# Output by pairs of batches: seven tokens of a run on one partition, one DMA for a pair, in an attention and soft-MoE kernel

## The chip, the cores and the metric

The kernel runs on one core of one Trainium2 chip. The metric is the device time of one execution in microseconds (us); the figure given for a kernel is the median over its timed runs. The engines are named as in the profile: PE (TensorE, matmuls; PEld its weight loads), DVE (VectorE), ACT (ScalarE), POOL (GpSimd), SP (SyncE, which here does nothing but issue the output's DMAs). "Tile" is the library that lays out buffers and puts the waits between engines; the kernel asks it to keep the order of instructions as written.

## The reference

Attention over 8 batches, 12 heads, 448 tokens and a head size of 64, with a softmax that has an extra term in its denominator; then a soft mixture of experts over all 3,584 tokens with 8 experts of 4 slots each.

```python
scores = scale * np.matmul(q, k.transpose(0, 1, 3, 2))
m = np.max(scores, axis=-1, keepdims=True)
e = np.exp(scores - m)
attn = e / (np.sum(e, axis=-1, keepdims=True) + np.exp(-m) + 1e-09)
x = np.matmul(attn, v)             # then tokens to rows: [3584, 768]

logits = x @ phi                   # [3584, 32]
d = np.exp(logits - logits.max(0)) # over tokens
d /= d.sum(0, keepdims=True) + 1e-09
slot_input = (d.T @ x).reshape(E, S_per_e, D)
for e in range(E):
    h = np.maximum(slot_input[e] @ w1[e], 0.0)
    slot_out[e] = h @ w2[e]
c = np.exp(logits - logits.max(1)) # over slots
c /= c.sum(1, keepdims=True) + 1e-09
out = c @ slot_out                 # [3584, 768], float32, 11.01 MB
```

## The kernel before

**Tokens.** A batch's 448 tokens are 64 runs of 7 successive tokens: run p holds tokens 7p to 7p + 6. The seven are kept in four column groups. Groups 0, 1 and 2 have 128 columns: the first 64 are token i of each run (i = 0, 1, 2), the other 64 are token 4 + i. Group 3 has 64 columns, token 3.

**Main loop.** For 48 steps (8 batches of 6 pairs of heads, line 532 on) the kernel transposes q and k, takes row maxima (L226, L233), exponentials (L299), multiplies by v (L324), normalizes, and turns the result for the logits (L367 to L372). After the last pair of a batch the lambdas of `P(b)` run, spread over the next steps: logits, a running softmax over tokens into `acc`, and for the softmax over slots the step `c_turn` (L450 to L457). It transposes the exponentials `cd` of the batch, so that the slots lie on partitions (32 of them for each of the four groups: 128 partitions) and tokens on columns, copies that to `cT[:, b, :]` (L453), and leaves the reciprocal of each token's sum in `crec[:, b, 0:4]` (L455 to L457). `crec` has tokens on partitions: column i belongs to group i, rows 0 to 63 to the first 64 tokens of the group, rows 64 to 127 to the others. For the last batch this is `last[3]`, called after the hidden layers.

**Weights.** w1 and w2 of the experts, 16 pieces of 128 x 6144 bf16, are loaded on POOL's queue during the main loop: 11 into buffers of a pool `wpool` with 11 buffers (L594), five into parts of `R` whose contents are no longer needed.

**Experts.** After the main loop: `hidden(0)` and `hidden(1)` (L624, L626) for experts 0 to 3 and 4 to 7, `last[3]()`, `turn(0)`, `turn(1)` (transposes L631, copies L632), `slots(0)`, `slots(1)` (L639, copies L644 and L645), and a selection by masks (L664 to L669) which leaves in `slot_out` the 32 slots' outputs, four times, on partitions 0 to 31, 32 to 63 and so on. The tile `wt`, the buffer of the first expert's w1, holds these intermediates.

**Output (L672 to L695).** For each batch four PSUM tiles of two banks are taken, one for each token group. Eight matmuls (two halves of 384 columns, outer; four groups, inner) multiply `cT`'s 32 rows of a group by `slot_out`. Then the four tiles are scaled by `crec` into a buffer `o` in SBUF: groups 0 and 2 by ACT (L688), 1 and 3 by DVE (L690). Group 3 has 64 rows. So `o` has tokens 0 to 3 of run p on partition p, and tokens 4 to 6 on partition 64 + p. Two DMAs on SP's queue take a batch to the output: L694 from partitions 0 to 63 (four tokens, 12,288 contiguous bytes for each partition), L695 from partitions 64 to 127 (three tokens, 9,216 bytes). The first batch goes in two cuts of two and one or two tokens, so there are 18 DMAs. `o` takes the pool's buffers after `wt`: those that held w1 of experts 1 to 7 and w2 of expert 0. Tile gives the output's DMAs eight semaphores in turn; the ninth and later issues wait also for the landing of the eighth before.

Of the kernel before, what the change touches and what calls it, by code (L numbers as in the profile page):

```python
# [30 lines left out]
def kernel(  # L31
# [10 lines left out]
    nc = tc.nc  # L42
    B, H, S, D = q.shape
    DD = H * D
    NS = moe_phi.shape[1]
    E = moe_w1.shape[0]
    SE = NS // E
    F = moe_w1.shape[2]
    KC = DD // 128
    FK = F // 128  # L50
    ND = DD // 2
# [7 lines left out]

    const = ctx.enter_context(tc.tile_pool(name="const", bufs=1))  # L60
    keep = ctx.enter_context(tc.tile_pool(name="keep", bufs=1))
    wpool = ctx.enter_context(tc.tile_pool(name="wpool", bufs=11))


    cT = keep.tile([128, B, 128], BF16, name="cT")
    crec = keep.tile([128, B, 4], F32, name="crec")
    acc = keep.tile([128, KC + 1, NS], F32, name="acc")

# [1 line left out]
    identf = const.tile([128, 128], F32, name="identf")  # L70
# [27 lines left out]
    w_sb = {}  # L98
# [10 lines left out]
    def load_half(i, z, t=None):  # L109

        if t is not None:
            w_view(i, t)
        n = (KC if halves[i][0] == "w1" else FK) // 2
        load_part(i, z * n, (z + 1) * n)

    w_tile = lambda: wpool.tile([128, KC * F], BF16, tag="w", name="w_sb")
    for i in range(5):
        w_view(11 + i, R[:, i * KC * F:(i + 1) * KC * F])

    with ExitStack() as at:  # L120
# [6 lines left out]
        pb_ = lambda nm: psB.tile([128, 512], F32, tag="b", name=nm)  # L127
# [33 lines left out]
        for base in (0, 64):  # L161

            nc.gpsimd.affine_select(
                out=sel[base:base + 64], in_=sel[base:base + 64], fill=1.0,
# [215 lines left out]
        def P(b):  # L380
# [69 lines left out]
            def c_turn():  # L450
                ps = pa([128, 128], BF16, "ps_ct")
                nc.tensor.transpose(ps, flat(v["cd"][:, 0:4, :]), ident)
                nc.vector.tensor_copy(cT[:, b, :], ps)  # L453
                r = crec[:, b, :]
                nc.vector.reduce_sum(r, v["cd"][:, 0:4, :], axis=AX.X)  # L455
                nc.vector.tensor_scalar(r, r, 1e-9, None, op0=ALU.add)
                nc.vector.reciprocal(r, r)  # L457
# [36 lines left out]
        take = lambda z, n: ub[:, z:z + n]  # L494
# [2 lines left out]
        masks = [take(F + KC * NS + g * 4 * NS, 4 * NS).rearrange("p (r s) -> p r s", r=4) for g in range(2)]  # L497
        fold = take(F + (KC + 8) * NS, 2 * NS).bitcast(F32)
        hrec = psm.tile([128, 1], F32, name="hrec", bufs=1)
        last = P(B - 1)  # L500
        post[2 * NPAIR] = last[0]

# [25 lines left out]
        half_at = {s: i for i, s in enumerate((1, 4, 7, 10, 13, 16, 22, 25, 28, 31, 34))}  # L528
# [3 lines left out]
        for s in range(NPAIR + 1):  # L532
            for y in range(2):
                hs = 2 * s + y
                early = int(hs < 5)
                As(1)
                if s < NPAIR:
                    Bk(s, 2 * y)
                    As(early)
                    Bk(s, 2 * y + 1)  # L540
                As(1)
                if hs == 1:
                    W1(1)
                if hs < 5:
                    T(hs + 3)
                if y == 0:
                    if 0 <= s - 1:
                        for i in (2, 3):
                            AV(s - 1, i, range(3))
                else:  # L550
                    if 2 <= s < NPAIR - 6:
                        T(s + 6)
                    g = (s + 1) // 3
                    if (s + 1) % 3 == 0 and g < NG:
                        W2(g + 1)
                        W3(g + 1)
                    if s < NPAIR:
                        for i in (0, 1):
                            AV(s, i, range(3))
                if 2 * s + y in post:  # L560
                    post[2 * s + y]()
                if y and 0 <= s - 2 < NPAIR - 2:
                    PX(s - 2)
                if y == 0:
                    if 0 <= s - 1:
                        for i in range(4):
                            AV(s - 1, i, [3])
# [12 lines left out]
            g = (s + 9) // 3  # L580
            if s % 3 == 0 and g - 2 < NG:
                V(g - 2)
                if s and g - 1 < NG:
                    load(g - 1, "v")
            if s == 1 or (s and s % 3 == 0):
                if g < NG:
                    load(g, "q")
                    load(g, "k")
            if s % 3 == 1:
                if 1 < (s + 2) // 3 < NG:  # L590
                    W1((s + 2) // 3 + 1)
                if s == 1:
                    load(2, "v")
            if s in half_at:  # L594
                load_half(half_at[s], 0, w_tile())
            if s - 1 in half_at:
                load_half(half_at[s - 1], 1)
            for i, z0, z1 in part_at.get(s, ()):
                load_part(i, z0, z1)
# [7 lines left out]
        for g in range(2):  # L607

            nc.gpsimd.memset(masks[g], 0.0)
            o = masks[g][:, :, 16 * g:16 * g + 16].rearrange("p r (i k) -> p r i k", i=4)  # L610
# [17 lines left out]
        def turn(g):  # L628
            ps = psA.tile([128, FK, 128], BF16, tag="a", name="ps_ht")
            for kt in range(FK):  # L630
                nc.tensor.transpose(ps[:, kt, :], h[g][:, kt * 128:(kt + 1) * 128], ident)  # L631
            nc.vector.tensor_copy(hT[g], ps)  # L632

        def slots(g):
            pss = [pb_("ps_so") for _ in range(2)]
            for kt in range(FK):
                for half in range(2):
                    for i in range(4):
                        nc.tensor.matmul(pss[half][32 * i:32 * i + 32, 0:ND],  # L639
                                         hT[g][:, kt, 32 * i:32 * i + 32],  # L640
                                         w_sb["w2", 4 * g + i][:, kt, half * ND:(half + 1) * ND],
                                         start=(kt == 0), stop=(kt == FK - 1),
                                         skip_group_check=True)
            nc.scalar.copy(so[g][:, 0:ND], pss[0][:, 0:ND])  # L644
            nc.vector.tensor_copy(so[g][:, ND:DD], pss[1][:, 0:ND])  # L645

        hidden(0, h0)

        wt = w_tile()
        h1, so = wt[:, 0:F], [wt[:, 3 * F + g * DD:3 * F + (g + 1) * DD] for g in range(2)]  # L650
        h = [h0, h1]
        hT = [wt[:, (1 + g) * F:(2 + g) * F].rearrange("p (k s) -> p k s", k=FK) for g in range(2)]
        slot_out = wt[:, 3 * F + 2 * DD:3 * F + 3 * DD]
        hidden(1, h1)
        last[3]()
        turn(0)
        turn(1)
        slots(0)
        slots(1)
        for half in range(2):  # L660
            hs = slice(half * ND, (half + 1) * ND)
            ps = psA.tile([128, 512], F32, tag="a", name="ps_sel")
            for g in range(2):
                nc.tensor.matmul(ps[:, 0:ND], masks[g].rearrange("p r s -> p (r s)"), so[g][:, hs],  # L664
                                 start=(g == 0), stop=(g == 1))
# [3 lines left out]
                nc.scalar.copy(slot_out[:, hs], ps[:, 0:ND])  # L669


    with ExitStack() as ex:  # L672
        psO = ex.enter_context(tc.tile_pool(name="psO", bufs=4, space=PSUM))
        for b in range(B):
            o = wpool.tile([128, KC * F], BF16, tag="w", name="o_sb")[:, :].bitcast(F32)
            o = o.rearrange("p (i d) -> p i d", i=4)
            pss = [psO.tile([128, 2, 512], F32, tag="o", name="ps_o") for _ in range(4)]
            for half in range(2):
                for i in range(4):
                    m = 128 if i < 3 else 64  # L680
                    r = slice(32 * i, 32 * i + NS)
                    nc.tensor.matmul(pss[i][0:m, half, 0:ND], cT[r, b, 0:m],  # L682
                                     slot_out[r, half * ND:(half + 1) * ND], start=True, stop=True)
            for i in range(4):
                m = 128 if i < 3 else 64
                dst = o[0:m, i, :].rearrange("p (h d) -> p h d", h=2)
                if i % 2 == 0:
                    nc.scalar.mul(dst, pss[i][0:m, :, 0:ND], crec[0:m, b, i:i + 1])  # L688
                else:
                    nc.vector.tensor_scalar(dst, pss[i][0:m, :, 0:ND], crec[0:m, b, i:i + 1], None, op0=ALU.mult)  # L690
            ov = out[b * S:(b + 1) * S, :].rearrange("(p t) d -> p t d", t=7)
            cuts = [0, 2, 4] if b == 0 else [0, 4]
            for t0, t1 in zip(cuts, cuts[1:]):
                nc.sync.dma_start(out=ov[:, t0:t1, :], in_=o[0:64, t0:t1, :])  # L694
                nc.sync.dma_start(out=ov[:, 4 + t0:min(4 + t1, 7), :], in_=o[64:128, t0:min(t1, 3), :])  # L695


# [28 lines left out]
```

## Time and profile before

| what | us |
|---|---|
| median of 3 runs | 341.22 (340.12 to 342.4) |
| the profiled execution's own time | 341.64 |
| its span on the core | 339.9 |
| hidden layers end, turns of the last batch | about 291 |
| slots (L639) | 292.7 to 298.0 |
| first matmul of the output stage | 299.8 |
| first output DMA issued | 301.9 |
| last scaling ends | 324.7 |
| last output DMA issued, landed | 329.9, 338.6 |

A second table has the rows of the output stage and of the small steps before it, one instruction's mean from the groups of the profile:

| line | engine | what | count | mean ns |
|---|---|---|---|---|
| L682 | PE | 32 x 128 by 32 x 384 | 48 | 461 |
| L682 | PE | 32 x 64 by 32 x 384 | 16 | 500 |
| L688 | ACT | scaling, 128 x 768 | 16 | 897 |
| L690 | DVE | scaling, 128 x 768 | 8 | 1018 |
| L690 | DVE | scaling, 64 x 768 | 8 | 1001 |
| L453 | DVE | copy into cT, 128 x 128 | 8 | 224 |
| L457 | DVE | reciprocal, 128 x 4 | 8 | 178 |
| L632 | DVE | copy of a turned hidden layer, 128 x 1024 | 2 | 686 |
| L406 | PE | fp32 transpose, 128 x 128 | 8 | 325 |

The page's own list of DMA issues has the output in these groups (bytes of one, median us from issue to landing):

```profile
out_dram<-o_sb SPq DMA_DIRECT2D x7, 768.0 KB, 8.9
out_dram<-o_sb SPq DMA_DIRECT2D x7, 576.0 KB, 8.3
out_dram<-o_sb SPq DMA_DIRECT2D x3, 384.0 KB, 4.8
out_dram<-o_sb SPq DMA_DIRECT2D x1, 192.0 KB, 5.1
```

How to read such a profile: it is one execution. The page cuts the span into 40 equal slices and gives, for each engine, a digit for its busy share in tenths; PEclk is the granted clock of TensorE, DMA the mean busy share of the 16 DMA engines, GB/s what they moved. A timeline row has the start, the time, engine and line, the operation, the tiles out<-in with shapes, and in brackets how long the engine had been idle before it and what ended that. "SPq" is SP's sequencer, where a DMA's issue is recorded. A windows row gives the same sums for any stretch.

### The profile page before, as it was taken

To read this page: it belongs to the slowest core of one execution; us is meant where nothing else is said; L and a number is where in the kernel's file an instruction comes from. 1 tells how busy PE (TensorE), PEld (TensorE's weight loads), DVE (VectorE), ACT (ScalarE), POOL (GpSimd) and SP (SyncE) were. 2 spreads that over 40 slices of the span, in tenths; PEclk is the share of its full clock that TensorE was granted. 3 is DMA by queue.
4 is the path that set the end of the run, shared out by engine and by line. 5 is a ranking of instruction groups with operands and counts; after the bars stand their busy time and mean duration, and the time that the engine had idled before them with its cause. 6 is when DMAs were issued, how large, how long until landed. Compare 5 with 4: busy or idle time off the path is not lost.

```text
span 339.9 us, 12092 instructions
## 1 busy us (share of the span) xinstructions
PE 295.1 (87%) x5040; PEld 167.7 (49%) x5040; DVE 264.6 (78%) x609; ACT 253.5 (75%) x547; POOL 198.8 (58%) x399
## 2 busy tenths in 40 slices
PE   3898999999999999999999999999999868977800
PEld 1344556556564656555656555565645433522200
DVE  5789998989998999899989899998893563255520
ACT  2476799998999799889989998998899842255410
POOL 8742777969587777777785969586567350000000
PEclk9999999999999999999999999999999985975555
DMA  7990999999999999099999999997344999839996
GB/s 93 125 128 0 159 186 175 179 194 137 201 146 180 159 171 148 9 171 151 176 172 179 148 185 153 180 147 126 48 70 74 157 211 208 150 79 268 353 361 235
DMA packets 42870, 54.30 MB, mean 160 GB/s; under 512 B 2752, under 2 KB 35520, under 8 KB 41920
## 3 DMA queue, kind: packets, MB, share of 16 engines
q0 software_dynamic: 41376, 42.52, 81.4%
q1 hardware_dynamic: 1440, 11.01, 9.8%
q8 instruction: 39, 0.64, 0.7%
q14 instruction: 15, 0.12, 0.1%
HBM read 85.03 MB, written 11.01 MB: 283 GB/s over the span
## 4 chain that ended last, share of the span: by engine, by line
PE 43%; DVE 25%; ACT 12%; issue 6%; DMA 6%; POOL 3%; DVEq 0%; POOLq 0%; ACTq 0%
DVE mx L226 15%; PE ps_av L324 8%; PE ps_b L294 6%; PE ps_a L222 6%; DMA R<-in_k_dram 5%; ACT R L299 5%; PE ps_t L200 5%; PE ps_b L296 4%; PE ps_o L682 3%; ACT R L203 2%; PE ps_h L624 2%; ACT o_sb L688 2%; PE ps_s L447 2%; DVE mx L233 2%; ACT R L370 2%
## 5 line engine op out<-in xcount | busy, mean ns | idle before, releaser
L226 DVE TENSOR_REDUCE mx<-ps_a 128x1 f32<-128x448 f32 x288 | 160.8, 615 | 12.3 <-PE ps_a L222 11.1
L299 ACT ACTIVATE R<-ps_b 128x448 bf16<-128x448 f32 x336 | 157.9, 555 | 13.8 <-PE ps_b L296 9.3
L294 PE MATMUL ps_b<-R 64*128 64x448 bf16 (+1 forms) x384 | 82.2, 357 | 0.9 <-ACT R L370 0.2
L296 PE MATMUL ps_b<-mT,sel 64*128 64x448 bf16 (+1 forms) x384 | 78.2, 352 | 0.0
L222 PE MATMUL ps_a<-R 64*128 64x448 bf16 x288 | 68.6, 364 | 6.0 <-DVE mx L226 4.3
L349 POOL TENSOR_TENSOR R<-ubuf,rec 128x384 bf16<-128x384 f32 x44 | 36.2, 824 | 55.2 <-DVE rec L346 53.0
L324 PE MATMUL ps_av<-R 128*128 128x65 bf16 (+1 forms) x1536 | 64.5, 196 | 1.5 <-DVE ubuf L336 1.4
L324 PEld LDWEIGHTS <-R 128*128 128x128 bf16 (+1 forms) x1536 | 50.3, 100 | 28.0 <-issue 24.0
L200 PEld LDWEIGHTS <-R 64*64 64x64 bf16 x1344 | 30.3, 113 | 19.9 <-issue 8.6
L370 ACT CAST R<-ps_x 128x512 bf16<-128x512 f32 x47 | 28.0, 597 | 13.9 <-PE ps_x L367 13.9
L200 PE MATMUL ps_t<-ident,R 64*64 64x64 bf16 x1344 | 31.2, 196 | 7.9 <-DMA R<-in_q_dram 4.3
L294 PEld LDWEIGHTS <-R 64*128 64x128 bf16 (+1 forms) x384 | 19.2, 97 | 27.8 <-issue 23.1
L296 PEld LDWEIGHTS <-sel 64*128 64x128 bf16 (+1 forms) x384 | 21.1, 97 | 23.1 <-issue 15.6
L233 DVE TENSOR_REDUCE mx<-ps_a 128x1 f32<-128x448 f32 x48 | 29.8, 621 | 0.7 <-PE ps_a L231 0.5
L203 ACT COPY R<-ps_t 128x896 bf16<-128x896 bf16 x20 | 18.3, 916 | 11.3 <-PE ps_t L200 11.3
L336 ACT COPY ubuf<-ps_av 128x455 f32<-128x455 f32 x44 | 24.6, 560 | 1.8 <-PE ps_av L324 1.0
L222 PEld LDWEIGHTS <-R 64*128 64x128 bf16 x288 | 17.8, 94 | 14.6 <-issue 3.8
L682 PE MATMUL ps_o<-w_sb,cT 32*128 32x384 bf16 x64 | 18.2, 470 | 5.8 <-ACT o_sb L688 5.1
L690 DVE TENSOR_SCALAR o_sb<-ps_o,crec 128x768 f32<-128x768 f32 (+1 forms) x16 | 15.5, 1010 | 9.4 <-PE ps_o L682 9.4
L688 ACT ACTIVATE o_sb<-ps_o,crec 128x768 f32<-128x768 f32 x16 | 13.5, 897 | 11.5 <-PE ps_o L682 11.5
L355 POOL TENSOR_TENSOR R<-ubuf,rec 128x128 bf16<-128x128 f32 x44 | 17.6, 400 | 3.7
L367 PE MATMUL ps_x<-ident,R 128*128 128x128 bf16 x192 | 18.8, 219 | 0.4 <-DVE R L355 0.4
(115 smaller groups left out, 371.6 us busy)
## 6 DMA issues: line engine op xcount, KB each, us to landing
w_sb<-in_moe_w_dram POOLq DMA_DIRECT2D x22, 768.0 KB, 8.8
R<-in_v_dram POOLq DMA_DIRECT2D x32, 192.0 KB, 4.6
out_dram<-o_sb SPq DMA_DIRECT2D x7, 768.0 KB, 8.9
R<-in_q_dram POOLq DMA_DIRECT2D x15, 336.0 KB, 7.3
R<-in_k_dram POOLq DMA_DIRECT2D x15, 336.0 KB, 8.2
out_dram<-o_sb SPq DMA_DIRECT2D x7, 576.0 KB, 8.3
R<-in_moe_w_dram POOLq DMA_DIRECT2D x4, 768.0 KB, 8.3
R<-in_moe_w_dram POOLq DMA_DIRECT2D x1, 1344.0 KB, 13.1
```

What stands on the lines that cost most here:

```text
L200: nc.tensor.transpose(ps[r, a, c:c + 64], src[r, pl, tok * D:(tok + 1) * D], ident[r, r])
L203: nc.scalar.copy(t, ps)
L222: nc.tensor.matmul(pss[hl][:, 0:S], t[r, 0, i * 128:(i + 1) * 128], t[r, 1, :], start=True, stop=True)
L226: nc.vector.reduce_max(mx[g][:, c:c + 1], pss[hl][:, 0:S], axis=AX.X)
L233: nc.vector.reduce_max(mx[g][:, c:c + 1], ps[:, 0:S], axis=AX.X)
L294: nc.tensor.matmul(outs[hl], t[rs[hl], 1, cols], t[rs[hl], 0, :], start=True, stop=False)
L296: nc.tensor.matmul(outs[hl], sel[rs[hl], 2 * pl + hl:2 * pl + hl + 1].to_broadcast([64, m]), mT[mg(n)][rs[hl], :], start=False, stop=True)
L299: nc.scalar.activation(e, p[:, 0:S], AF.Exp, scale=scale)
L324: nc.tensor.matmul(o, eT[n, i, hl][:, qc], vp[g % 2][:, 2 * pl + hl, i, 0:W65], start=(i == 0 and u == 0 and hl == 0), stop=(i == 3), skip ...
L349: eng.tensor_mul(x[:, 0:3, c:c + 128].rearrange("p i (h d) -> p i h d", h=2), u[:, 0:6, 0:D].rearrange("p (i h) d -> p i h d", h=2), rec[: ...
L370: nc.scalar.copy(xT[:, pb, :], ps)
L682: nc.tensor.matmul(pss[i][0:m, half, 0:ND], cT[r, b, 0:m], slot_out[r, half * ND:(half + 1) * ND], start=True, stop=True)
```

## The change

`cT` is laid out by pairs of batches, `[128, 4 pairs, 2 halves of a group, 2 batches, 64 runs]`, so that for a token and a pair the 128 runs of the two batches are 128 successive columns. In the output loop, now over four pairs, token t of both batches is one matmul pair of 128 rows. A partition holds one run's seven tokens (21,504 contiguous bytes; partitions 0 to 63 the even batch, 64 to 127 the odd one), in a group of four and a group of three PSUM tiles. Tokens 0 to 3 use the rows of groups 0 to 3 and the first half of columns, tokens 4 to 6 those of groups 0 to 2 and the second half. One DMA of 128 partitions takes a pair out; the first pair goes in three cuts, of tokens 0 and 1, 2 and 3, and 4 to 6. There are 6 output DMAs instead of 18, 56 matmuls instead of 64, and 28 scalings instead of 32, all of 128 rows.

The reciprocals have then to lie with a pair's runs on partitions: four fp32 matmuls against an identity of 64 x 64 move `crec`'s quadrants into PSUM, and two copies take them to `cscale`, after `turn(1)` and before `slots(0)`.

The pool of 11 weight buffers becomes one tile `W` of 11 x 6144 columns with fixed slices; the output's pairs lie in it one behind the other from the second slice on.

```diff
-    wpool = ctx.enter_context(tc.tile_pool(name="wpool", bufs=11))
-    cT = keep.tile([128, B, 128], BF16, name="cT")
+    cT = keep.tile([128, B // 2, 2, 2, 64], BF16, name="cT")
...
-    w_tile = lambda: wpool.tile([128, KC * F], BF16, tag="w", name="w_sb")
+    W = keep.tile([128, 11 * KC * F], BF16, name="W")
+    w_tile = lambda i: W[:, i * KC * F:(i + 1) * KC * F]
...
-                nc.vector.tensor_copy(cT[:, b, :], ps)
+                nc.vector.tensor_copy(cT[:, b // 2, :, b % 2, :], ps.rearrange("p (h j) -> p h j", h=2))
...
+        cscale = take(F + (KC + 10) * NS, 8 * B).bitcast(F32).rearrange("p (h b i) -> p h b i", h=2, i=4)
...
         turn(1)
+        for half in range(2):
+            ps = pb_("ps_cs")
+            r = slice(64 * half, 64 * half + 64)
+            for b2 in range(2):
+                nc.tensor.matmul(ps[64 * b2:64 * b2 + 64, 0:2 * B], identf[r, r], crec[r, b2::2, :],
+                                 start=True, stop=True)
+            nc.vector.tensor_copy(cscale[:, half].rearrange("p b i -> p (b i)"), ps[:, 0:2 * B])
         slots(0)
...
+        for bp in range(B // 2):
+            o0 = KC * F + bp * 14 * DD
+            o = W[:, o0:o0 + 14 * DD].bitcast(F32).rearrange("p (t d) -> p t d", t=7)
+            ov = out[2 * bp * S:2 * (bp + 1) * S, :].rearrange("(p t) d -> p t d", t=7)
+            for t0, t1 in (0, 4), (4, 7):
+                pss = [psO.tile([128, 2, 512], F32, tag="o", name="ps_o") for _ in range(t0, t1)]
+                for hf in range(2):
+                    for t in range(t0, t1):
+                        r = slice(32 * (t - t0), 32 * (t - t0) + NS)
+                        nc.tensor.matmul(pss[t - t0][:, hf, 0:ND], cT[r, bp, t0 // 4, :, :].rearrange("p b j -> p (b j)"),
+                                         slot_out[r, hf * ND:(hf + 1) * ND], start=True, stop=True)
+                for t in range(t0, t1):
+                    dst = o[:, t, :].rearrange("p (h d) -> p h d", h=2)
+                    c = cscale[:, t0 // 4, bp, t - t0:t - t0 + 1]
+                    if t % 2 == 0:
+                        nc.scalar.mul(dst, pss[t - t0][:, :, 0:ND], c)
+                    else:
+                        nc.vector.tensor_scalar(dst, pss[t - t0][:, :, 0:ND], c, None, op0=ALU.mult)
+            cuts = [0, 2, 4, 7] if bp == 0 else [0, 7]
             for t0, t1 in zip(cuts, cuts[1:]):
-                nc.sync.dma_start(out=ov[:, t0:t1, :], in_=o[0:64, t0:t1, :])
-                nc.sync.dma_start(out=ov[:, 4 + t0:min(4 + t1, 7), :], in_=o[64:128, t0:min(t1, 3), :])
+                nc.sync.dma_start(out=ov[:, t0:t1, :], in_=o[:, t0:t1, :])
```

More of the change, by code (lines that the diff above doesn't have):

```diff
@@ L594 @@
             if s in half_at:
-                load_half(half_at[s], 0, w_tile())
+                load_half(half_at[s], 0, w_tile(half_at[s]))
             if s - 1 in half_at:
@@ L647 @@
         hidden(0, h0)
-        wt = w_tile()
+        wt = w_tile(0)
         h1, so = wt[:, 0:F], [wt[:, 3 * F + g * DD:3 * F + (g + 1) * DD] for g in range(2)]
@@ L673 @@
         psO = ex.enter_context(tc.tile_pool(name="psO", bufs=4, space=PSUM))
[L674 to L692, printed above, removed]
```

## The prediction

> **What bounds the kernel now.** I read four views in this order: the page's slices, the timeline of the end, the windows of the output stage, and the DMA issues with the trace's packet records. The slices first (40 slices of 8.5 us; the last five cover 297.4 to 339.9 us):
>
> ```profile
> PE   3898999999999999999999999999999868977800
> PEclk9999999999999999999999999999999985975555
> DMA  7990999999999999099999999997344999839996
> GB/s 93 125 128 0 159 186 175 179 194 137 201 146 180 159 171 148 9 171 151 176 172 179 148 185 153 180 147 126 48 70 74 157 211 208 150 79 268 353 361 235
> ```
>
> The change touches only the output stage and two small steps before it. In that stage TensorE runs at half clock and ends two slices before the span does, while the DMA digits read 9, 9, 9, 6. So the stage is to be read as a transfer of the output, and the question is what sets its rate: 79, 268, 353, 361, 235 GB/s.
>
> The timeline shows where the stage starts and what closes the span:
>
> ```profile
> 299.83 1.16 PE L682 MATMUL ps_o<-w_sb,cT 32*128 32x384 bf16 x8 [0.65 <-DVE w_sb L667]
> 301.94 0.52 SPq L694 DMA_DIRECT2D out_dram<-o_sb  x1
> 302.50 0.59 SPq L695 DMA_DIRECT2D out_dram<-o_sb  x1
> ...
> 322.73 1.69 ACT L688 ACTIVATE o_sb<-ps_o,crec 128x768 f32<-128x768 f32 x2 [1.44 <-PE ps_o L682]
> ...
> 329.93 1.74 SPq L695 DMA_DIRECT2D out_dram<-o_sb  x1
> ```
>
> The last eviction is over by 324.7 us, the last issue comes at 329.93 and lands at 338.59; 1.3 us of closing work follow, and the span is 339.9. From 324.7 on no engine computes. Making evictions cheaper would therefore gain nothing by itself; a faster drain, or bytes that start earlier, would.
>
> The windows (per row: start and end, length, busy time of PE, PEld, DVE, ACT, POOL, then clock, DMA share, GB/s) say why the drain is slow:
>
> ```profile
> 303.10:305.10 2.00, 1.47 (x7) 0.49 (x7) 1.14 (x2) 1.17 (x2) 0.00 (x0) 0.50 1.00 200
> 309.00:311.00 2.00, 1.62 (x6) 0.45 (x6) 0.80 (x2) 0.81 (x2) 0.00 (x0) 0.50 1.08 229
> 320.00:322.00 2.00, 1.30 (x5) 0.36 (x4) 1.56 (x2) 1.29 (x2) 0.00 (x0) 0.50 1.01 399
> 324.00:326.00 2.00, 0.00 (x0) 0.00 (x0) 0.70 (x1) 0.42 (x1) 0.00 (x0) 0.50 1.04 407
> ```
>
> All 16 DMA engines are busy in all four, yet the rate is 200, 229, 399 and 407 GB/s. The packet records (start, length and bytes of each packet) tell the difference. An output packet is one partition's run: 12,288 bytes from partitions 0 to 63 (L694), 9,216 from 64 to 127 (L695). Between 309.0 and 311.9 nearly all 16 packets in flight are of L694; each then takes 0.84 to 1.01 us, and together they make 203 GB/s in the microsecond at 310. With five or fewer of the other kind beside them the mean rate is 288 to 356; with eight and eight it is 388. An undisturbed packet takes 0.460 us (L694) or 0.347 us (L695): 26.7 and 26.6 bytes per ns, so 16 engines could do 425 GB/s. L694's packets average about 0.59 us from 316 on, while L695's stay at 0.347 beside them. So what is short is not the destination, which both kinds share, but something that belongs to the source half: about 8 engines' worth (8 x 26.7 = 213 GB/s) for each 64 partitions. L694 carries 6.29 of the 11.01 MB, and 6.29 MB / 213 GB/s = 29.5 us of the 35.1 us that the packets last (303.1 to 338.25).
>
> **The change, part by part.**
>
> *One DMA of 128 partitions.* Eighteen issues become six; every DMA now draws on both halves, with 8 rows per engine, and the halves carry 5.5 MB each. At 26.6 bytes/ns an engine needs 8 x 0.24 us = 1.9 us for a two-token DMA (6,144-byte rows), 8 x 0.356 = 2.85 for three tokens, 8 x 0.82 = 6.5 for a pair (21,504 bytes, 2.75 MB). Total 25.8 us at 425 GB/s. The bounds: 425, and 361, the best 8.5-us slice, which gives 7.6 us a pair. Nearest is the 399 to 407 of the windows where the halves happened to balance, without any order to keep them so; I take 410, 6.7 us a pair. The issue: 64 rows take SP 0.52 us unhindered, for 128 I allow twice that (later issues take 1.4 to 2.4 us, with earlier DMAs still pending); nothing but output stands behind it on SP, and 1.17 us pass from an issue to its first packet (301.94 to 303.11). I keep 1.2 and carry up to 0.5 more in the range.
>
> The Trainium skill speaks against this part: its page "SBUF — State Buffer", section "A bandwidth-pool intuition that's wrong (but worth ruling out)", lists about 358 GB/s between HBM and one core, below the 436 it gives for DMA and SBUF, and the slice of 361 looks like that limit. By that rule a pair would take 7.7 us and the gain fall to about 3 us; the 399 and 407 GB/s of the windows differ from it. Its page "DMA: Bandwidth & Descriptors", section "Rules for kernel authors", would have it the other way: transfers on disjoint partition halves serialize, so the old drain would run at one half's rate throughout (52 us by the 213 GB/s above, where 35 were measured); the same two windows, with both halves in flight, differ from that too.
>
> *Supply.* A pair has 7 tokens, in a group of four and one of three; evictions fall from 32 to 28, all of 128 partitions. From the timeline's rows: ACT's scaling takes 0.90 us, the second of a pair starting 0.80 after the first, DVE's 1.02 and 0.93; a matmul starts 0.05 after its buffer is free, the second half's first matmul starts about 0.45 after the first half's last, and the eviction 0.53 after that. Group one ends as before at 302.5 (ACT) and 302.8 (DVE). Tokens 4 to 6 find their buffers at 301.7, 301.9 and 302.5; second half at 303.0, ACT 303.5 to 304.4 and 304.3 to 305.2. Pair 1's first four: last buffer 305.3, ACT from 306.3 to 308.0; its last three end at 310.7. So a pair takes 5.5 us where two batches took 6.26, below the 6.7 of a drain: from pair 1 on, DMA is the bound and the evictions' saving is hidden. Issues fall at 301.9, about 303, 305.3, 310.8, 316.2 and 321.7. If a group of three costs what four cost (3.13), pairs come every 6.26 us, still under the drain.
>
> *Coarser grain.* From the second pair on (pair 1), no byte leaves before the pair's last scaling. What hides that wait is the drain of the pair before; the first pair's three cuts are drained by about 310, so at pair 1 the cover is gone and the DMA engines idle until its first packet. The price stands in the sum.
>
> *The turned factors (cscale).* Four fp32 matmuls of 64x16 on TensorE and two copies of 128x16 on DVE, between the turns and slots(0). DVE's copies stand behind L632, which ends at 293.27, and before L645 at 295.56: covered by 2.3 us. The matmuls wait for L457 (ends 292.05); slots(0) started at 292.73, when its first copy landed, so 0.7 us of cover. The nearest row is the fp32 transpose L406, 0.30 us for 128x128 with 0.14 of load: four serial are 0.56 (loads alone) to 1.8, so the delay is 0 to 1.1 us. The new ones have an eighth of the columns; I take 0.4, all on the path. Without the cover it would be 1.1.
>
> *One tile for the weights.* GpSimd's instructions stay one for one, and the slots of the weights lie end to end as the buffers did. The output lies on w1 of experts 1 to 7, last read at 290.9, nine us before the first scaling. The copies of L453 write two runs of 64 in place of 128: 0.22 us, eight times, among DVE work of 265 us; I take 0, with 8 x 0.2 = 1.6 at the most if each became twice as long, and nothing to gain.
>
> *The sum*, against the profiled execution. First issue 301.9 + 0.4 = 302.3, first packet 303.5; the first pair's DMAs drain by about 310.2 (2.75 MB at 410 GB/s, supplied in time). Pair 1 is issued at 310.8 + 0.4 = 311.2, its packets start at 312.4: an idle of about 2 us. Then 3 x 6.7 = 20.1 us, to 332.5, and 1.6 from the last packet to the span's end (338.25 to 339.9): 334.1. That is 5.8 us under 339.9. The profiled execution took 341.64, 1.74 over its span and 0.42 above the median of 341.22; so the time is 334.1 + 1.74 - 0.42 = **335.4 us**, 1.7% less.
>
> **The rivals.**
>
> *A common limit near 360 GB/s.* For it: the slices 353 and 361 with DMA digits of 9. Against: the windows above. Drain 3 x 7.65 from 312.4 gives 335.4, span 337.0, time 338.3, 0.9% less: within what can be told.
>
> *Halves in turn, slower.* Nothing in this trace shows which rows of a 128-row output each engine gets. If the engines went through the rows together, partitions 0 to 63 first, every moment would be like 310 us: 203 to 233 GB/s (233 is the mean with 16 packets of L694 in flight), 47 to 54 us from 303.5, span 352 to 359, time 353.7 to 360.6. It decides as soon as the rate from 303.5 on falls under 11.01 MB / 34.7 us = 317 GB/s. Against it: GpSimd's 128-partition loads reach 211 GB/s landed, with twice as much read, and show no trouble, though that is not proof.
>
> *Late supply.* A group of three costs as much as one of four, so pair 1 ends at 312.2 + 0.4 instead of 311.2, and twice 1.2 us pass before its first packet: 315.0, then 20.1 and 1.6, span 336.7, time 338.0.
>
> **How the numbers follow.** About 1% (3.4 us) is what can be told from no change. Full-rate drain 0.72 (0.71 of it faster by more than 1%); common limit 0.13 (0.03 faster, 0.10 same); halves in turn 0.08, slower; late supply 0.07 (0.03 faster, 0.04 same). With 0.01 same from the first: faster 0.77, same 0.15, slower 0.08. The low end: 425 GB/s (19.4 in place of 20.1), hidden factors (0.4) and half of the idle (1.0), so 333.3, and 0.4 for the spread of the runs: 332.9. The high end takes in late supply and the common limit: 339.0.
>
> **What would show it.** Right: six issues on SP; pair packets near 0.8 us each in all halves; 400 GB/s or more from about 312 to 332; an idle of 1 to 2 us in the DMA just before; evictions over by about 322. The common limit would show packets of 0.95 us, all alike; halves in turn, packets of 1.6 us or more at about 210 GB/s. The forecast is wrong if the engine-side work before 299.8 moves by more than 1 us, or if the idle before pair 1 exceeds 4 us.

## The result and the profile after

The changed kernel takes 331.41 us (median of 4 runs, 330.56 to 331.77) against 341.67 for the one before in the same comparison: a ratio of 0.971, 95% interval 0.969 to 0.974. The forecast was 335.4, 332.9 to 339.0. Direction and mechanism held; the gain is 10.3 us where 5.8 were forecast, and the time lies 1.5 us below the range.

The profiled execution took 331.65 us, its span is 329.88 (339.86 before). The slices of the page, now 8.25 us each:

```profile
PE   3898999999999999999999999999999985895620
PEclk9999999999999999999999999999999998597555
DMA  6990999999999999479999999999636399984997
GB/s 80 143 130 3 138 195 168 194 180 155 179 151 186 153 185 146 70 83 183 149 203 144 166 153 205 150 179 139 94 50 98 50 185 208 209 146 167 417 417 334
```

At the same half clock and the same DMA digits of 9, the last slices read 417, 417, 334 in place of 353, 361, 235. The timeline of the stage (start, length, engine, line, tiles):

```profile
299.22 0.50 PE L693 MATMUL ps_o<-W,cT 32*128 32x384 bf16 x8 [0.66 <-DVE W L676]
299.81 1.69 ACT L699 ACTIVATE W<-ps_o,ubuf 128x768 f32<-128x768 f32 x2 [1.05 <-PE ps_o L693]
...
301.55 0.82 PE L693 MATMUL ps_o<-W,cT 32*128 32x384 bf16 x5 [0.31 <-ACT W L699]
...
302.08 1.69 ACT L699 ACTIVATE W<-ps_o,ubuf 128x768 f32<-128x768 f32 x2 [0.59 <-PE ps_o L693]
...
308.36 0.33 SPq L704 DMA_DIRECT2D out_dram<-W  x1
...
315.77 1.69 ACT L699 ACTIVATE W<-ps_o,ubuf 128x768 f32<-128x768 f32 x2 [0.59 <-PE ps_o L693]
...
317.48 0.33 SPq L704 DMA_DIRECT2D out_dram<-W  x1
```

Eight matmuls take 0.50 us where the same row read 1.16 before; the next group's scaling starts 2.27 us after the first one's (3.14 before); the second pair is issued at 308.36; scaling is over by 317.5, and the rest is drain. The DMA issues (bytes of one, median us to landing) and the windows:

```profile
out_dram<-W SPq DMA_DIRECT2D x3, 2688.0 KB, 9.7
out_dram<-W SPq DMA_DIRECT2D x2, 768.0 KB, 3.8
out_dram<-W SPq DMA_DIRECT2D x1, 1152.0 KB, 5.1
```

```profile
301.80:303.80 2.00, 1.20 (x7) 0.30 (x3) 1.02 (x1) 1.69 (x2) 0.00 (x0) 0.50 1.02 415
308.00:309.00 1.00, 0.84 (x7) 0.12 (x5) 0.04 (x1) 0.41 (x2) 0.00 (x0) 0.50 0.36 148
309.40:313.40 4.00, 2.53 (x14) 0.75 (x14) 2.52 (x3) 2.91 (x4) 0.00 (x0) 0.50 1.01 430
321.40:325.40 4.00, 0.00 (x0) 0.00 (x0) 0.00 (x0) 0.00 (x0) 0.00 (x0) 0.50 1.01 430
```

From its first two microseconds on the drain runs at 415 to 430 GB/s in these full windows (200 at its start before), with one gap, in which the second window lies: no packet is in flight from 308.56 to 309.19, before the second pair's first. Packets of 21,504 bytes take 0.799 to 0.821 us (5th to 95th percentile, median 0.804): 26.7 bytes per ns for each engine, the undisturbed figure of before.

The 9.98 us of span fall into four parts: the output stage starts 0.61 sooner (299.83 to 299.22); from its first matmul to the first packet 0.69 less (3.28 to 2.59); the packets last 8.33 less (35.14 to 26.81); from the last packet to the end 0.36 less (1.61 to 1.25).

### The profile page after: what moved, and what is told of

The parts are those of the page before. It is cut to its first block, busy times and chain, and to the rows that moved or that the text cites. A ratio compares the mean times of both kernels' runs of the same rounds, so it can differ in the third digit from the quotient of the medians.

```text
span 329.9 us, 12091 instructions
## 1 busy us (share of the span) xinstructions
PE 287.5 (87%) x5040; PEld 165.9 (50%) x5040; DVE 261.0 (79%) x607; ACT 253.3 (77%) x547; POOL 198.2 (60%) x399
## 4 chain that ended last, share of the span: by engine, by line
PE 48%; DVE 24%; ACT 12%; issue 6%; DMA 4%; POOL 1%; ACTq 0%; POOLq 0%; DVEq 0%
DVE mx L226 15%; PE ps_av L324 10%; PE ps_b L294 8%; PE ps_a L222 7%; PE ps_b L296 5%; PE ps_t L200 5%; ACT R L299 5%; DMA R<-in_k_dram 3%; ACT R L203 2%; PE ps_h L625 2%; PE ps_s L447 2%; ACT W L699 2%; DVE mx L233 2%; ACT R L370 2%; PE ps_so L640 2%
## 5 line engine op out<-in xcount | busy, mean ns | idle before, releaser
L222 PEld LDWEIGHTS <-R 64*128 64x128 bf16 x288 | 17.8, 94 | 14.4 <-issue 3.6
L106 POOL DMA_DIRECT2D W<-in_moe_w_dram x22 | 17.9, 814 | 0.9 <-issue 0.9
L231 PE MATMUL ps_a<-R 64*64 64x448 bf16 x96 | 17.5, 360 | 0.6 <-DVE mx L226 0.6
L106 POOL DMA_DIRECT2D R<-in_moe_w_dram x15 | 10.7, 713 | 11.9 <-PE ps_b L296 5.1
```

What stands on the lines that cost most here:

```text
L106: gdma(out=w_sb[(kind, e)][:, z0:z1, :], in_=src[:, z0:z1, :])
L222: nc.tensor.matmul(pss[hl][:, 0:S], t[r, 0, i * 128:(i + 1) * 128], t[r, 1, :], start=True, stop=True)
```

## The experiments

Since the output stage starts at different times in different executions (298.2 to 302.7 us over all profiles below), most readings are of the "stage": from its first matmul to the span's end, 40.03 us before and 30.66 after.

### Is it the source half, the number of rows, or their length?

**e1_two_halves**

```diff
-                nc.sync.dma_start(out=ov[:, t0:t1, :], in_=o[:, t0:t1, :])
+                for p in (0, 64):
+                    nc.sync.dma_start(out=ov[p:p + 64, t0:t1, :], in_=o[p:p + 64, t0:t1, :])
```

> The changed kernel, with each of its six output DMAs split into one of partitions 0 to 63 and one of partitions 64 to 127; rows, bytes, order of the pairs and all compute stay. Theory A (what was short before is the source half: packets of one half share about 213 GB/s): 64-row DMAs of one half are slow whenever nearly all 16 engines sit in that half, so packets of 21,504 bytes spread between 0.80 and 1.6 us, the drain runs at 350 to 390 GB/s in place of 427, and the time rises by 3 to 6 us, to 334.5 to 337.5 us. Rival B (the longer rows, 21,504 bytes in place of 12,288 and 9,216, made the drain faster): packets stay at 0.80 us and the time within 0.5 us of 331.4. Rival C (fewer and larger issues on SP): twelve issues in place of six cost at most 6 x 0.35 us on SP, which is hidden: no change.

Measured: 348.19 us (4 runs), ratio to before 1.019, 1.011 to 1.027. The changed kernel with its DMAs cut at partition 64 is slower than the kernel before. Rows, bytes and compute being those of the changed kernel, B falls. C falls too: SP's last issue ends at 323.2 us, and the packets go on to 344.7, at a mean of 257 GB/s from there. The stage is 47.33 us; packets of 21,504 bytes take 0.80 to 1.88 us (5th to 95th percentile), and the windows show busy DMA engines at little more than one half's rate:

```profile
312.00:316.00 4.00, 2.51 (x13) 0.43 (x10) 2.62 (x3) 2.82 (x4) 0.00 (x0) 0.50 1.10 252
324.00:328.00 4.00, 0.00 (x0) 0.00 (x0) 0.00 (x0) 0.00 (x0) 0.00 (x0) 0.50 0.93 253
```

Theory A has the right sign, but its size was wrong (stage and time grow by 17 us in place of 3 to 6): it took the rates of the kernel before (350 to 390) for those of any two halves in turn. e9 and e12 go into that.

**e2_lows_first**

```diff
-                nc.sync.dma_start(out=ov[:, t0:t1, :], in_=o[:, t0:t1, :])
+                nc.sync.dma_start(out=ov[0:64, t0:t1, :], in_=o[0:64, t0:t1, :])
+            late.append((ov, o))
+        for ov, o in late:
+            nc.sync.dma_start(out=ov[64:128], in_=o[64:128])
```

> The changed kernel, with the output DMAs of partitions 0 to 63 of all four pairs issued as they become ready, and those of partitions 64 to 127 of all four after them, so that one half alone is in flight most of the time. Theory A (about 213 GB/s for each half): 5.5 MB at 213 GB/s twice is 51.7 us from the first packet at 301.8, packets of 21,504 bytes near 1.6 us, span about 355, time about 356 us. Rival B (long rows) and a limit of the destination (360 to 427 GB/s whatever the half): drain of 26 to 31 us, time 331 to 337 us. Late supply of the upper halves cannot explain more than 1 us: pair 3 is scaled by 317.5.

Measured: 360.43 us (one run), span 358.6, stage 58.36; A gave 355 for the span. The mechanism is the one of A: packets of 21,504 bytes take 1.675 us in the median, twice 0.804, with 16 in flight for all but 5.5 of 53.8 us, and the mean rate is 204 GB/s from first to last packet, a little under the 213 that A took. (A window counts a packet in the one where it starts, so short windows scatter.)

```profile
304.00:306.00 2.00, 1.35 (x7) 0.25 (x7) 0.73 (x2) 1.41 (x2) 0.00 (x0) 0.50 0.97 200
332.00:336.00 4.00, 0.00 (x0) 0.00 (x0) 0.00 (x0) 0.00 (x0) 0.00 (x0) 0.50 1.02 210
340.00:344.00 4.00, 0.00 (x0) 0.00 (x0) 0.00 (x0) 0.00 (x0) 0.00 (x0) 0.50 1.06 220
```

The same rate holds while the engines compute (304 us) and long after (340 us), and for the lower half (304) and the upper (332 on).

**e6_middle**

```diff
-                nc.sync.dma_start(out=ov[:, t0:t1, :], in_=o[:, t0:t1, :])
+                nc.sync.dma_start(out=ov[32:96, t0:t1, :], in_=o[32:96, t0:t1, :])
+            late.append((ov, o))
+        for p in (0, 96):
+            for ov, o in late:
+                nc.sync.dma_start(out=ov[p:p + 32], in_=o[p:p + 32])
```

> The changed kernel, with the output DMAs of partitions 32 to 95 (64 rows, half of them from each half) issued as the pairs become ready, then those of partitions 0 to 31 of all pairs, then those of 96 to 127. Theory A (the source half is what is short, not the number of rows of a DMA): the 64-row DMAs of the middle run at full rate, packets of 21,504 bytes at 0.80 us with 16 in flight; those of 0 to 31 and then of 96 to 127 at about 1.6 us. Span: middle done by about 321, then twice 2.75 MB at 213 GB/s = 25.8 us, near 348; time about 350. Rival B (a DMA of 64 rows is slow whatever its partitions, as two engines would share something per row count): the middle's packets take 1.6 us as well, span near 354.

Measured: 352.2 us (one run), span 350.4. The middle's DMAs have 64 rows, like the slow ones, but take them from both halves:

```profile
310.20:313.20 3.00, 1.84 (x9) 0.63 (x9) 2.37 (x3) 2.41 (x4) 0.00 (x0) 0.50 0.98 416
314.80:317.80 3.00, 1.42 (x6) 0.31 (x5) 2.33 (x3) 2.41 (x4) 0.00 (x0) 0.50 0.95 401
325.00:328.00 3.00, 0.00 (x0) 0.00 (x0) 0.00 (x0) 0.00 (x0) 0.00 (x0) 0.50 1.12 229
```

Their packets take about 0.81 us at 401 to 416 GB/s; those of partitions 0 to 31 at 325 us take 1.68. So it is the half from which a DMA reads, not the number of its rows: B falls. The Trainium skill, "SBUF — State Buffer", section "Door 1: The DMA port swizzle (why `[64,N]` ≈ `[32,N]`)", assigns partitions to 16 ports by a formula in which 0 to 63 have 8 and 32 to 95 all 16; both figures here agree with it.

### Why equal halves in turn were slower than the kernel before

**e9_fine_halves** (24 DMAs)

```diff
-            cuts = [0, 2, 4, 7] if bp == 0 else [0, 7]
+            cuts = [0, 2, 4, 7]
             for t0, t1 in zip(cuts, cuts[1:]):
-                nc.sync.dma_start(out=ov[:, t0:t1, :], in_=o[:, t0:t1, :])
+                for p in (0, 64):
+                    nc.sync.dma_start(out=ov[p:p + 64, t0:t1, :], in_=o[p:p + 64, t0:t1, :])
```

> The changed kernel with DMAs of 64 partitions, first half and second half in turn as in e1_two_halves, but every pair cut in three (tokens 0 and 1, 2 and 3, 4 to 6): 24 DMAs with rows of 6,144 and 9,216 bytes in place of 12. It asks why e1 was slower (47.3 us from the first output matmul to the span's end) than the kernel before (40.0). Theory A (the engines must drift apart by about one DMA's share of four packets before they spread over both halves; with rows of 21,504 bytes that is 3 to 6 us, with 6,144 about 1 to 2): the rate climbs to 370 GB/s or more within some 10 us of the first packet, and the stage takes 34 to 38 us. Rival B (halves in turn cost the same whatever the length of a turn): 250 to 315 GB/s throughout, 45 us or more. Rival C (SP's issues of 0.5 to 2.6 us become the bound): 24 issues without a pause, 16 engines not full, 40 us or more.

Measured: 346.92 us (one run), stage 45.52. If the time from the first packet to the last one's end is cut in five equal parts ("fifths"), the packets make 256, 259, 274, 279 and 261 GB/s. Theory A's rate does not come: halves in turns of equal length stay slow with short rows as with long ones. The signs of C are partly there: the 24 issues follow one another without a pause, to 338.7 us, and the engines are not always full.

```profile
301.35 37.39 SPq L705 DMA_DIRECT2D out_dram<-W  x24
318.00:322.00 4.00, 0.00 (x0) 0.00 (x0) 0.00 (x0) 0.00 (x0) 0.00 (x0) 0.50 0.98 272
```

But C can explain only a part. On average 14.4 of 16 packets are in flight, so the missing ones amount to 4.0 of the 41.4 us of packets, and at 425 GB/s all of it would take 25.9. The rest is packets that take longer: those of 6,144 bytes 0.33 us in the mean, where 0.234 is the undisturbed time.

**e12_unequal**

```diff
-            cuts = [0, 2, 4, 7] if bp == 0 else [0, 7]
-            for t0, t1 in zip(cuts, cuts[1:]):
-                nc.sync.dma_start(out=ov[:, t0:t1, :], in_=o[:, t0:t1, :])
+            for p, t0, t1 in (0, 0, 4), (64, 0, 3), (0, 4, 7), (64, 3, 7):
+                nc.sync.dma_start(out=ov[p:p + 64, t0:t1, :], in_=o[p:p + 64, t0:t1, :])
```

> The changed kernel with four DMAs of 64 partitions for each pair, of unequal rows: first half 12,288 bytes (tokens 0 to 3), second half 9,216 (0 to 2), first half 9,216 (4 to 6), second half 12,288 (3 to 6). It asks why the kernel before, with 12,288 and 9,216 in turn, reached 350 to 390 GB/s late in its drain while equal halves in turn (e1, e9) stayed at 250 to 315. Theory A (turns of unequal length let engines that share a half part company): the rate climbs above 340 GB/s in the second half of the drain, and the stage takes 36 to 42 us. Rival B (unequal turns do nothing): 250 to 315 GB/s throughout, 44 us or more; then the cause of the difference stays open.

Measured: 343.92 us (one run, in which the stage started only at 302.7), stage 39.43, although its first packet comes 1.24 us later after the first matmul than the changed kernel's. The fifths read 233, 340, 385, 377 and 269 GB/s; the kernel before has 247, 285, 360, 369, 305.

```profile
306.60:309.60 3.00, 1.97 (x9) 0.46 (x9) 1.73 (x3) 2.36 (x3) 0.00 (x0) 0.50 1.14 229
322.00:326.00 4.00, 0.00 (x0) 0.00 (x0) 0.00 (x0) 0.00 (x0) 0.00 (x0) 0.50 1.02 402
```

The drain begins at one half's rate and climbs, as before the change. So in these runs turns of unequal length let the halves overlap and equal ones hardly do (one run each of e9 and e12; e12's rows and the number of its DMAs, 16, lie between those of e9, 24 DMAs with shorter rows, and of e1, 12 with longer ones, so neither explains its faster drain): the rates of the kernel before came with its four tokens on one half and three on the other. In that kernel the packet sizes tell the halves apart: of the packets in flight, the half with fewer has 2.2 on average in the second fifth, 4.7 in the third and 5.6 in the fourth, as the rate climbs from 285 to 369 GB/s. So the halves come to be in flight side by side; why unequal turns bring that about is argued, as the packet records here have no engine.

### Why the supply was faster than forecast

**e3_wide** (the kernel before)

```diff
-                    m = 128 if i < 3 else 64
                     r = slice(32 * i, 32 * i + NS)
-                    nc.tensor.matmul(pss[i][0:m, half, 0:ND], cT[r, b, 0:m],
+                    nc.tensor.matmul(pss[i][:, half, 0:ND], cT[r, b, :],
```

> The kernel before, with group 3's matmuls 128 columns of cT wide in place of 64 (the upper 64 rows of that PSUM tile are computed and not used); everything else as before. Theory A: the 64-column weights kept the fourth matmul of each half from running beside the other three (0.27 us later at full clock, 0.40 at half), and this, not the size of the groups, made the cadence 3.13 us for four scalings; with 128 columns the cadence falls to about 2.3 us, as in the changed kernel, the first scaling starts 0.37 us sooner after the first matmul, and the last one ends about 6 us sooner. The time falls by only 0.4 to 1 us, to 340.7 to 341.3, because the drain bounds the stage. Rival B (the cadence came down because a group of three is smaller, or because of the new order): the cadence stays at 3.1 us and the time at 341.7.

Measured: 341.33 us (10 runs), ratio 0.998, 0.995 to 1.001: no difference that the runs can tell. The profile tells it:

```profile
298.23 0.50 PE L681 MATMUL ps_o<-w_sb,cT 32*128 32x384 bf16 x8 [0.65 <-DVE w_sb L667]
298.81 1.69 ACT L687 ACTIVATE o_sb<-ps_o,crec 128x768 f32<-128x768 f32 x2 [1.04 <-PE ps_o L681]
...
301.21 1.69 ACT L687 ACTIVATE o_sb<-ps_o,crec 128x768 f32<-128x768 f32 x2 [0.71 <-PE ps_o L681]
```

Eight matmuls in 0.50 us in place of 1.16, the first scaling 0.58 after the first matmul in place of 0.96, and the next group 2.40 after that in place of 3.14. The last scaling ends 20.32 us after the first matmul (24.87 before), 4.6 us sooner where about 6 were expected, yet the packets last 35.1 us as they did: as forecast, cheaper evictions (the scalings out of PSUM) alone gain nothing but the earlier first packet. The stage is 39.57, 0.46 less.

**e5_narrow** (the changed kernel; tokens 3 and 6 of the odd batches are left out)

```diff
+                        m = 64 if t in (3, 6) else 128
-                        nc.tensor.matmul(pss[t - t0][:, hf, 0:ND], cT[r, bp, t0 // 4, :, :].rearrange("p b j -> p (b j)"),
+                        nc.tensor.matmul(pss[t - t0][0:m, hf, 0:ND], cT[r, bp, t0 // 4, :, :].rearrange("p b j -> p (b j)")[:, 0:m],
...
+                    m = 64 if t in (3, 6) else 128
-                    dst = o[:, t, :].rearrange("p (h d) -> p h d", h=2)
+                    dst = o[0:m, t, :].rearrange("p (h d) -> p h d", h=2)
```

> The changed kernel, with the last matmul of each group (tokens 3 and 6) 64 columns of cT wide in place of 128, so that each group mixes widths as before the change did; for these two tokens the odd batch of a pair is left out (64 of 128 rows are neither multiplied nor scaled; the DMA carries what lies there). DMAs are the same. Theory A (the 64-column weights made the old cadence, and the cadence was mis-sized in the forecast): a group takes 3.1 us in place of 2.28, a pair about 5.9 to 6.2 in place of 4.56, the second pair is issued 1.5 to 2.0 us later after the first output matmul (9.14 us now), the idle before its packets grows from 0.6 to about 2 us, and the time rises by 1.3 to 2.0 us, to 332.7 to 333.4. The later pairs stay covered by the drain of 6.45 us. Rival B (width does not matter, the smaller group does): cadence 4.56 and the time at 331.4.

Measured: 333.6 us (4 runs), ratio to before 0.973, 0.965 to 0.981: the times alone don't tell it from the changed kernel with its 0.971. The profile does: stage 32.22, 1.56 more than the changed kernel.

```profile
299.46 1.16 PE L694 MATMUL ps_o<-W,cT 32*128 32x384 bf16 x8 [0.65 <-DVE W L676]
300.43 1.69 ACT L701 ACTIVATE W<-ps_o,ubuf 128x768 f32<-128x768 f32 x2 [1.43 <-PE ps_o L694]
...
303.11 1.68 ACT L701 ACTIVATE W<-ps_o,ubuf 128x768 f32<-128x768 f32 x2 [0.99 <-PE ps_o L694]
...
305.78 1.69 ACT L701 ACTIVATE W<-ps_o,ubuf 128x768 f32<-128x768 f32 x2 [0.99 <-PE ps_o L694]
```

The old 1.16 is back, groups follow each other by 2.67 instead of 2.28, a pair takes 5.35 in place of 4.56, and the second pair is issued 10.71 us after the first matmul in place of 9.14. The DMA then stands idle, from 309.2 to 311.0:

```profile
309.00:311.00 2.00, 1.74 (x7) 0.33 (x5) 0.51 (x1) 1.14 (x2) 0.00 (x0) 0.50 0.03 11
```

Theory A holds: one 64-column weight among the 128-column ones sets the pace of a group. The expected 3.1 us for a group was too much: 3.13 is the time of four scalings, and a pair here has seven. At 0.78 us for each, as before the change, seven would take 5.5.

### What is left, and the scatter

**e4_cuts** (12 DMAs)

```diff
-            cuts = [0, 2, 4, 7] if bp == 0 else [0, 7]
+            cuts = [0, 2, 4, 7]
```

> The changed kernel, with every pair cut in three DMAs (tokens 0 and 1, 2 and 3, 4 to 6), twelve DMAs in place of six. Theory A: what is left of the coarse grain is the idle of 0.6 us before the second pair's packets; with cuts those bytes start about 2 us sooner, so the idle goes and the time falls by 0.4 to 0.7 us, to about 330.8; rows of 6,144 and 9,216 bytes move at 26.0 to 26.6 bytes per ns per engine against 26.7, so 0.3 us may be given back. Rival B (long rows matter): packets at 24 bytes per ns or less and the time 2 us or more higher, 333.4 and up.

Measured: 331.71 us (4 runs), ratio to before 0.970, 0.964 to 0.976, against 0.971: no difference. The gap at 308.6 is gone, and the packets last 26.54 us in place of 26.81, so more than half of the 0.6 us is given back; from the last packet to the end it is 1.51 us in place of 1.25. Stage 30.63.

**e7_second_cut**

```diff
-            cuts = [0, 2, 4, 7] if bp == 0 else [0, 7]
+            cuts = [[0, 2, 4, 7], [0, 4, 7], [0, 7], [0, 7]][bp]
```

> The changed kernel, with the second pair's DMA cut in two (tokens 0 to 3, then 4 to 6); seven output DMAs. Theory A: the second pair's first bytes are issued about 2.3 us sooner, before the first pair is drained, so the idle of 0.6 us goes; the large packets stay: 0.3 to 0.6 us less, about 331.0, at the edge of what can be told. Rival B (the idle is not on the path, as something later bounds the drain): no change at all in the time from the first output matmul to the span's end, 30.7 us now.

Measured: 332.38 us (4 runs, 330.6 to 333.69), ratio to before 0.969, 0.962 to 0.977: not to be told from the changed kernel. The profile shows what theory A says: no gap, packets for 26.14 us, stage 29.98.

**e8_before_again** (the kernel before, unchanged)

> The kernel before, unchanged: a second profile of it. Theory A (the 0.6 us by which the output stage started sooner in the profile of the changed kernel is scatter of the main loop): its first output matmul lies between 298.2 and 300.3 us, and 40.0 us pass from there to the span's end, with the halves of the output as unequal as before. Rival B (the one tile for the weights sped up the main loop): its first output matmul comes at 299.8 or later again.

Measured: 340.17 us (one run); first output matmul at 298.22, stage 40.17. B falls: the start moves by 1.6 us between two profiles of the same kernel, so the 0.61 of the changed kernel's is no effect that can be shown.

**e10_after_again** (the changed kernel) and **e11_second_cut_again** (e7's edit), five rounds on one chip

> The changed kernel, unchanged, to be compared with the next run on the same chip: ratio to before 0.969 to 0.973; from the first output matmul to the span's end 30.7 us.

> The same as e7_second_cut (the second pair in two DMAs), on the same chip as the changed kernel: the stage took 29.98 us there against 30.66. Theory A: 0.7 us less than the changed kernel in the median, 0.2%; the scatter of the main loop (298.2 to 300.3 us at the start of the output stage so far) is larger, so five rounds may not tell it. Rival B: the shorter stage was itself scatter, and it takes 30.5 us or more here.

Measured: 332.28 us for the changed kernel (ratio 0.973, 0.970 to 0.976, stage 30.47) and 330.64 for the one with the second cut (ratio 0.968, 0.965 to 0.970, stage 29.97). All six runs of the second (329.91 to 331.35) are below all six of the first (331.43 to 333.56). The stage is 0.5 us shorter, where A has 0.7, and under the 30.5 of B. The medians are 1.6 us apart; so are the two profiled executions, and there the rest lies before the stage (it started at 300.36 and 299.28), where the kernels' instructions are the same. Whether that rest is chance stays open. The second cut is the best version run here, and 0.5 to 0.7 us of its lead are explained by the profiles.

## Why the prediction was wrong

The mechanism was the one forecast, *one DMA of 128 partitions*: six issues, pair packets near 0.8 us, 400 GB/s or more, a gap before the second pair, and then a drain without a break. Of the causes named, e1, e2 and e6 leave only the source half. The rivals "a common limit near 360 GB/s" and "halves in turn, slower" are refuted by windows of 430 GB/s. What the second would have cost is seen in e2, where one half is in flight at a time: a span of 358.6 us, where that rival had 352 to 359.

What failed is the sum, with a span of 334.1 forecast and 329.9 measured. Term by term:

| term of the sum | forecast us | measured us | difference |
|---|---|---|---|
| first output matmul (299.83, and 0.4 for cscale) | 300.2 | 299.2 | -1.0 |
| first matmul to the issue of the second pair | 11.0 | 9.14 | -1.9 |
| that issue to its first packet | 1.2 | 0.83 | -0.4 |
| drain of three pairs | 20.1 | 19.44 | -0.7 |
| last packet to the end | 1.6 | 1.25 | -0.35 |

**Supply** is the step that failed: the time to the issue of the second pair, 11.0 us forecast and 9.14 measured. It took the spacing of matmuls from the rows of before: "the second half's first matmul starts about 0.45 after the first half's last", "Group one ends as before", hence "So a pair takes 5.5 us". That spacing belonged to the 64-column weight of group 3, which the change itself removes. In the trace of before the sign was there: three weights of a half are loaded together, and the fourth and the next half's three each 0.27 or 0.28 us later, as are their matmuls.

```profile
299.82 0.10 PEld L682 LDWEIGHTS <-cT 32*128 32x128 bf16 x3 [1.04 <-DVE w_sb L667]
300.10 0.10 PEld L682 LDWEIGHTS <-cT 32*64 32x64 bf16 x1 [0.17 <-issue]
300.37 0.10 PEld L682 LDWEIGHTS <-cT 32*128 32x128 bf16 x3 [0.17 <-issue]
300.64 0.10 PEld L682 LDWEIGHTS <-cT 32*64 32x64 bf16 x1 [0.17 <-issue]
```

In the changed kernel the second half's first matmul starts together with the first half's last (both at 301.55), so the wait is gone from every group, while the 0.53 from there to the scaling (302.08) stands as forecast. A pair takes 4.56 us. e3 takes the delay away in the old kernel, and e5 brings it back in the new, where a pair then takes 5.35, near the forecast 5.5, and the second pair's issue comes 1.57 us later, close to the 1.9 of the table. The forecast's own logic made this term count: the second pair's cover is gone, so each microsecond of supply up to that point is on the path. Later pairs are covered, as it said. The idle before the second pair's packets was 0.63 us where about 2 were forecast.

**The issue** was mis-sized the same way, by 0.4: for 128 rows the forecast kept 1.2 us to the first packet and allowed SP twice the 0.52 us of 64 rows. It took SP 0.33, and 0.83 to the first packet.

**cscale**: hidden, not 0.4. The eight passes of the four fp32 matmuls are over within 0.30 us, before the first copy of the turned layer ends:

```profile
291.39 1.27 DVE L633 COPY W<-ps_ht 128x1024 bf16<-128x1024 bf16 x2
291.57 0.30 PE L664 MATMUL ps_cs<-crec,identf 64*64 64x16 f32 x8
292.12 0.34 PE L640 MATMUL ps_so<-W 128*32 128x384 bf16 x3 [0.25 <-DVE W L633]
```

L640 starts 0.73 us after L633; before, the same two were 0.75 apart. The other 0.6 us of that row can't be told from scatter (e8).

**Drain**: 19.44 us is 425 GB/s, the upper bound given; the 410 was drawn down by windows in which the halves only happened to balance. The Trainium skill, "SBUF — State Buffer", section "A bandwidth-pool intuition that's wrong (but worth ruling out)", lists 358 GB/s between HBM and one core; as an estimate from that figure this drain would have taken 23 us. The 19.44 measured differ from it; every run here used one core. The rule of its page "DMA: Bandwidth & Descriptors", section "Rules for kernel authors", that transfers on disjoint halves serialize, came closer than the prediction allowed: e9's equal halves in turn make 256 to 279 GB/s, a fourth to somewhat over a third above the 204 of one half alone (e2). One reading of the packets was too tight: of the 48 packets of L694 that start between 309.0 and 311.9 us, 29 take 0.84 to 1.01 us, not each of them. The 203 GB/s beside it holds.

**Last packet to the end**: SP closes with waits for the DMAs, some 0.06 us each in the traces. Before, the wait that the last landing (338.59) released was followed by six more, from 338.67 to 338.97; now it is the last one, at 328.99. That is the 0.36 us, and the six waits could be seen in the trace of before.

**One tile for the weights** cost nothing that shows, and **late supply** did not come. The range was too narrow at its low end: it took off half of the idle (1.0 us), where about 1.6 went, and left no room for the main loop's scatter. With Supply as it was measured, 1.86 us less, the forecast would have been 333.5, inside the range; the rest is the table's smaller rows, which all went the same way.

## What to carry to other kernels

Where output is bound as here, give every output DMA partitions from both halves of SBUF, 0 to 63 and 64 to 127 (425 GB/s over the last three pairs, against 204 with one half at a time); where 64 rows must do, take 32 to 95 rather than 0 to 63 (e6), and do not trust two DMAs in turn to overlap (e1, e9). When a duration is carried over from the old trace, ask whether the change removes what made it: a cadence is not a property of the group's size until its matmuls' starts have been read one by one. Where a bound moves from a drain to the supply of its first full piece, cut that piece: the second pair in two DMAs took the gap out.

## What the runs showed of the hardware

In these traces a matmul on a 32-row group with 64 weight columns did not start beside those on other row groups with 128: it came 0.27 us later at full clock (300.10 after 299.83, before), 0.40 at a granted clock of 0.50 (306.07 after 305.67). With equal widths, and buffers free, the four started within 0.02 us (after and e3).

An output DMA of 128 rows occupied SP for 0.33 to 0.38 us when few were pending, one of 64 rows for 0.47 to 0.61; the first packet came 0.87 us after the first issue with 128 rows, 1.17 to 1.25 with 64. Issues of one-half DMAs with others pending took up to 2.66 us (e1, e2, with up to four pending in e1); twelve of 128 rows, also with up to four pending, at most 0.73 (e4). What SP waits for there was not tried.
